# Fused attention and gated layer on one core: transfers and their issue moved, zero products added to the first maxima

## The chip, the cores and the metric

The kernel runs on one core of a Trainium2 chip. Its engines are TensorE (PE: matrix products into PSUM; PEld is its weight load), VectorE (DVE), ScalarE (ACT), GpSimd (POOL) and SyncE (SP). In this kernel SP only issues DMAs, POOL issues some as well. The engines run side by side, each in the order of its own instructions, and wait for each other by semaphores. The metric is the device time of one execution in microseconds, lower is better.

## The reference

```python
def _attn_ref(q, k, v):                       # 8 batches, 8 heads, 1152 rows, 64 columns
    q_pool = q.reshape(B, H, S // 2, 2, D).mean(axis=3)
    scores = scale * np.matmul(q_pool, k.transpose(0, 1, 3, 2))
    scores = scores - np.max(scores, axis=-1, keepdims=True)
    attn = np.exp(scores)
    attn = attn / (np.sum(attn, axis=-1, keepdims=True) + 1e-09)
    return np.matmul(attn, v)

def _moe_ref(x, w_in, w_out):                 # x: 4608 tokens x 512, w_in 512 x 2048, w_out 2048 x 512
    h = x @ w_in
    g = h - np.tanh(h)
    return g @ w_out
```

The attention's output, heads side by side, is x.

## The kernel before, in words

**Attention** goes over 32 pairs of heads (8 batches of 4 pairs), `pi` in the code. Keys and queries of a pair arrive as `raw` (SP, function `load`); ScalarE rounds them to a high part `hi` (tile kq_h, functions `high_keys` and `high`), and the low part `lo` (tile kq_l) comes from ScalarE's negative copy (`minus_high`) and an adding DMA on POOL's queue (`low`). In the same way `minus_keys` and the DMA of `differences` make differences of keys and sum the two halves of the queries. A product of scores is three products of high and low parts. Before a pair's scores, maxima of its rows are taken from products of the high parts alone: 12 by `max_part` (TensorE, then a VectorE reduction `mx`) and two by `max_last` for the last 64 rows of both heads, whose queries SP copies into a tile of their own, `q_last` (function `last_queries`, at the end of `high`). `max_row` brings the maxima by VectorE, `m_dram` and two DMAs into the row `m_row`, which the scores subtract by a product with `sel`. For pair 0 a product with `eye` (`turn`) does this instead.

The order of a pair is written out as a string of tokens. `A` and `B` are the scores of the two halves of the queries (9 tiles of keys each; ScalarE's exponential follows, POOL adds exponentials in threes), `V` the products with the values, `m`, `L` and `l` the maxima of a later pair (`L` and `l` are `max_last`), `O` the sums of exponentials (ScalarE's copy `s_s` follows), `R` the second `turn`. The number behind the colon is the PSUM bank, of which there are four; `bank_111` to `bank_114` in an order listing are banks 0 to 3. Everything else hangs on places: `add(pi, place, f)` runs f after score number `place` of pair pi, or, from NS = 18 on, after its V number place - 18. So the place of an `add` sets where f's instructions stand on every engine, SP's queue included. SP issues its DMAs in this order and stops at each one that has to wait.

**Weights.** `W` converts a tile of w_in or w_out, which come as 64-bit numbers, to a high and a low part, one tile a pair: loads w_raw and w_off, token `T` (`begin` by ScalarE, `finish` by VectorE, six instructions, two DMAs to wi_dram or wo_dram).

**Reciprocals and x.** The sums go to s_dram; once a batch is through, `fetch_sums` and `reciprocals` (VectorE) write r_dram. x of a chunk of 512 tokens is fetched from x_dram into `x_l`, the reciprocals, spread over 64 rows, into `x_r`; `times`, `high` and `low` scale it and split it. For the first chunk this is spread over pairs 17 to 24.

**The second part** goes over 9 chunks in 16 steps each (n counts them all): `hidden` (12 products into ps_h), `shrink` (ScalarE squares and tanh, VectorE a polynomial, POOL a mask), and two steps later `second` (12 products into ps_o) with the high and low part of g. The first two steps are done inside the last pair (token `H`, `early_step`), with their weights in the raw tiles (`first_weights`) and their temporaries in kq_h and kq_l tiles. The other weights (w tiles) take the memory that the attention's pools give back.

Of the kernel before, what the change touches and what calls it, by code (L numbers as in the profile page):

```python
# [20 lines left out]
VALUES = "V:1 T:2 " + "V:1 " * 8 + "V:3 " * 4 + "m:0 m:1 m:2 " + "V:3 " * 5 + "m:1 L:0 l:3 O:2"  # L21
FIRST = (
    "A0:0 m0:1 A1:2 m0:3 A5:0 m0:1 A6:2 L0:3 A2:0 l0:1 A3:2 R:3 A7:0 m:1 A8:2 A4:0 m:1 B0:3 B1:2 B2:0 m:1 B5:3 B6:2 "
    "m:1 B7:0 B3:3 B4:2 m:1 B8:3 " + "V:1 " * 3 + "m1:0 m1:2 m1:3 " + "V:1 " * 4 + "m1:3 m1:0 m1:2 " + "V:1 " * 2 +
    "V:3 " * 2 + "m1:0 L1:1 l1:2 " + "V:3 " * 4 + "m:0 m:1 m:2 " + "V:3 " * 3 + "m:1 L:0 l:3 O:2")
# [3 lines left out]
LAST_BUT_ONE = PLAN + "V:1 T:2 " + "V:1 " * 8 + "T:0 " + "V:3 " * 9 + "O:2"  # L29
LAST = PLAN.replace("A7:1 ", "T:3 A7:1 ", 1) + "H:0 " + "V:3 " * 9 + "H:2 " + "V:3 " * 9 + "O:3"  # L30
# [29 lines left out]
def attention_ffn_kernel(  # L60
# [15 lines left out]
    P = 128  # L76
# [48 lines left out]
    class X:  # L125
# [8 lines left out]
        def fetch(self):  # L134
            sp.dma_start(self.l.bitcast(F32), x_dram[:, :, self.t0:self.t0 + self.n].rearrange("c p t -> p c t"))
# [87 lines left out]
    with ExitStack() as actx:  # L223
# [151 lines left out]

        def turn(pi, ta, tb, to):
# [119 lines left out]
        def early_step(to, places):  # L496
# [6 lines left out]
            b = lop.tile([P, LQ], F32R, name="kq_l")  # L503
            part = [a[:, 512 * i:512 * (i + 1)] for i in range(4)]
            m = a[:, 2048:2176].bitcast(mybir.dt.uint8)
            s.own = ((*part, m, bank[places][:, s.f]), b[:, 0:512], b[:, 512:1024])
# [17 lines left out]
        for pi in range(n_pair):  # L524
            if pi >= 2:
# [4 lines left out]
                else:  # L530
                    add(*((0, NS + 2) if pi == 3 else (pi - 3, 8)), load, pi)
# [12 lines left out]
        def begin_x():  # L544
            x0.append(X(0))
            x0[0].fetch()
# [13 lines left out]
        for f in range(2):  # L560
            add(n_pair - 1, 4, first_weights, f, (0, 1), "raw")
# [26 lines left out]
        def follow(pi, tokens, seen):  # L588

            for tok in tokens.split():  # L590
# [9 lines left out]
                elif what == "T":  # L600
                    w = work[len(made)]
                    made.append(w)
                    if seen["V"]:
                        w.begin(to, act)
                        at.setdefault((pi, NS + seen["V"] + 1), []).insert(0, w.finish)
                    else:
                        w.begin(to, dve)
# [58 lines left out]
    for ci in range(len(chunks)):  # L666
# [9 lines left out]
        for f in range(NF):  # L676
# [17 lines left out]
            if n == 4:  # L694
                fetch_sums(B - 1)
            if n == 6:
# [54 lines left out]
```

## Time and profile before

| | |
|---|---|
| median of 3 runs | 1601.51 us (1601.18 to 1602.08) |
| profiled execution | 1597.87 us, its span 1596.1 us |
| TensorE busy | 1544.3 us, 97% of the span |
| VectorE, ScalarE, POOL busy | 73%, 61%, 70% |

The page gives the busy time of each engine. TensorE is the longest, but a share over the whole span hides single places where it stands still; these are found by windows and by the idle time that a timeline notes in brackets before an instruction, with what ended it. PEclk is the clock that the chip granted to TensorE, 1 for 2.4 GHz. A time of a DMA in the chain of waits is from its issue to its landing.

### The profile page before, as it was taken

The numbers are of one execution on the slowest core, as the hardware profiler recorded it, in microseconds if no ns is written. First come the engines' busy times: TensorE is split into PE (matmuls) and PEld (weight loads), VectorE is DVE, ScalarE is ACT, GpSimd is POOL, SyncE is SP. The second block draws the span as 40 slices with busy tenths as digits, with TensorE's granted clock in tenths as the row PEclk, the third lists the DMA queues.
The fourth block names the chain that finished last, engine by engine and source line by source line (L and its number), as shares of the span: only waits on it lengthen the run. The fifth ranks groups of instructions, "written<-read, shape, count | busy, mean of one in ns | idle before, by whom it ended". The sixth has DMA issues, their size and how long they took to land.

```text
span 1596.1 us, 29936 instructions
## 1 busy us (share of the span) xinstructions
PE 1544.3 (97%) x11505; PEld 1193.5 (75%) x11505; DVE 1165.8 (73%) x1643; ACT 974.7 (61%) x1634; POOL 1112.7 (70%) x812
## 2 busy tenths in 40 slices
PE   7899999999979999999887999999999999999998
PEld 5577677767757677677676888888888888888886
DVE  5677777777757777777556777777777777777776
ACT  6476677667656676676444556565565556565554
POOL 7477787788757787787545666666667576666664
PEclk9999999999989999999998999999999999999999
DMA  5677678767768778776571101011010201020000
GB/s 160 179 225 213 200 216 238 184 215 220 221 184 219 200 219 226 192 215 175 213 308 36 66 14 67 7 35 43 10 67 14 67 14 67 14 67 14 27 0 27
DMA packets 92360, 202.66 MB, mean 127 GB/s; under 512 B 18232, under 2 KB 45240, under 8 KB 92216
## 3 DMA queue, kind: packets, MB, share of 16 engines
q1 hardware_dynamic: 83288, 156.04, 27.2%
q0 software_dynamic: 8928, 44.70, 15.1%
q8 instruction: 90, 1.47, 0.4%
q14 instruction: 54, 0.44, 0.1%
HBM read 134.25 MB, written 37.98 MB: 108 GB/s over the span
## 4 chain that ended last, share of the span: by engine, by line
PE 90%; DMA 5%; DVE 2%; POOL 1%; ACT 1%; issue 1%; SPq 0%; POOLq 0%; DVEq 0%; ACTq 0%
PE bank L50 44%; PE ps_h L50 24%; PE ps_o L50 23%; DMA w<-wo_dram 2%; DVE mx L50 1%; DMA q_last<-kq_h 1%; POOL sum L50 1%; DMA m_dram<-tr 0%; DMA rec<-s_dram 0%; DMA kq_l<-raw 0%; SPq L50 0%; DVE bank L50 0%; DMA raw<-in_qk_dram 0%; DMA w_raw<-in_w_out_dram 0%; DVE w_hl L50 0%
## 5 line engine op out<-in xcount | busy, mean ns | idle before, releaser
L50 DVE TENSOR_REDUCE mx<-bank 128x2 f32<-128x768 f32 x448 | 401.0, 925 | 171.2 <-PE bank L50 157.8
L50 POOL TENSOR_SCALAR g_m<-g_u 128x512 uint8<-128x512 f32 (+1 forms) x143 | 248.4, 1737 | 198.0 <-ACT g_u L50 183.7
L50 POOL TENSOR_TENSOR sum<-p,p 128x576 f32<-128x576 f32 x192 | 272.2, 1424 | 152.2 <-ACT p L50 152.2
L50 ACT ACTIVATE p<-bank 128x576 f32<-128x576 f32 x576 | 328.4, 659 | 24.1 <-PE bank L50 20.1
L50 PE MATMUL bank<-kq_h 64*128 64x288 f32 (+1 forms) x1920 | 288.5, 344 | 8.4 <-ACT kq_h L50 6.5
L50 PE MATMUL bank<-p,v 128*64 128x288 f32 x2304 | 293.9, 409 | 0.3 <-DVE mx L50 0.3
L50 POOL TENSOR_TENSOR sum<-sum,p 128x576 f32<-128x576 f32 x192 | 273.1, 1429 | 12.5
L50 PE MATMUL ps_o<-w,g_hi 128*128 128x512 f32 x792 | 244.0, 389 | 1.0 <-ACT g_hi L50 1.0
L50 PEld LDWEIGHTS bank<-p,v 128*64 128x64 f32 x2304 | 159.3, 137 | 114.5 <-issue 12.9
L50 POOL TENSOR_TENSOR g_lo<-g_s,g_hi 128x512 fp32r<-128x512 f32 (+1 forms) x143 | 184.1, 1287 | 84.3 <-ACT g_hi L50 84.3
L50 PEld LDWEIGHTS bank<-kq_h 64*128 64x128 f32 x1920 | 170.9, 185 | 74.6 <-DVE mx L50 25.9
L50 PE MATMUL ps_h<-x_h,w 128*128 128x512 f32 (+1 forms) x800 | 213.2, 389 | 13.9 <-DVE g_t L50 13.9
L50 ACT ACTIVATE g_u<-ps_h 128x512 f32<-128x512 f32 (+1 forms) x143 | 84.6, 592 | 230.9 <-PE ps_h L50 229.2
L50 DVE SCALAR_TENSOR_TENSOR ps_w<-g_u,ps_h 128x512 f32<-128x512 f32 (+1 forms) x143 | 99.0, 692 | 141.3 <-ACT g_t L50 141.3
L50 ACT ACTIVATE g_s<-g_u,pc 128x512 f32<-128x512 f32 (+1 forms) x286 | 190.5, 714 | 11.1
L50 PEld LDWEIGHTS ps_h<-x_h,w 128*128 128x128 f32 x800 | 150.1, 189 | 45.2 <-DVE g_t L50 14.3
L50 PEld LDWEIGHTS ps_o<-w,g_hi 128*128 128x128 f32 x792 | 148.5, 188 | 32.1 <-ACT g_hi L50 1.4
L50 PE MATMUL bank<-kq_l,kq_h 64*128 64x288 f32 x1152 | 170.6, 293 | 0.0
L50 PE MATMUL bank<-kq_h,kq_l 64*128 64x288 f32 x1152 | 170.4, 292 | 0.0
L50 PE MATMUL ps_o<-w,g_lo 128*128 128x512 f32 x396 | 154.4, 390 | 0.6 <-POOL g_lo L50 0.5
L50 DVE COPY_PREDICATED g_s<-g_m,g_t 128x512 f32<-128x512 uint8 (+1 forms) x143 | 108.0, 755 | 14.7
L50 DVE SCALAR_TENSOR_TENSOR g_s<-g_s,ps_w 128x512 f32<-128x512 f32 (+1 forms) x143 | 97.7, 683 | 17.5 <-DVE ps_w L50 3.7
(111 smaller groups left out, 2339.1 us busy)
## 6 DMA issues: line engine op xcount, KB each, us to landing
raw<-in_qk_dram SPq DMA_DIRECT2D x31, 864.0 KB
kq_l<-raw POOLq DMA_DIRECT2D x31, 864.0 KB, 7.5
v<-in_v_dram SPq DMA_DIRECT2D x32, 576.0 KB
raw<-in_qk_dram POOLq DMA_DIRECT2D x31, 544.0 KB, 11.0
x_dram<-o_s SPq DMA_DIRECT2D x32, 288.0 KB
x_l<-x_dram SPq DMA_DIRECT2D x9, 1024.0 KB
out_dram<-o_f SPq DMA_DIRECT2D x36, 256.0 KB
w_raw<-in_w_in_dram SPq DMA_DIRECT2D x16, 512.0 KB
```

The source lines that it names most:

```text
L50: i = f(*args, **kwargs)
```

## The change

1. Pair 0: `minus_high` and `low` of pair 1 move from the first values (places 18 and 19) to the sixth and eighth score (5 and 7); the load of pair 3 from place 20 to 18. One maximum of pair 1 moves from the scores to the values.
2. Nine first maxima use three banks, not four, and behind each stand one or two `warm`, two products of zeros each, into bank 3 (28 in all).
3. Token `T` moves ahead of the first V, and `finish` with it by one V. In the last pair the token is `D` (VectorE begins, as before).
4. x of the first chunk is fetched in four parts in pairs 10, 12, 14 and 16; x_r at the end of pairs 16, 18, 20 and 22. Its product with x moves from the end of the values to their first place (`product`: ScalarE copies x_r to bank 0, VectorE multiplies), `high` from place 34 to 28.
5. The raw tiles' weights are loaded at place 31 of pair 30, not at place 4 of pair 31.
6. The second early step keeps its g in two x_r tiles, not in a kq_l tile.
7. Sums and reciprocals of the last batch move from steps 4 and 6 to 30 and 32.

```diff
-VALUES = "V:1 T:2 " + "V:1 " * 8 + "V:3 " * 4 + "m:0 m:1 m:2 " + "V:3 " * 5 + "m:1 L:0 l:3 O:2"
+VALUES = "T:2 " + "V:1 " * 9 + "V:3 " * 4 + "m:0 m:1 m:2 " + "V:3 " * 5 + "m:1 L:0 l:3 O:2"
...
+        def warm(to):
+
+            for h in range(2):
+                pe.matmul(bank[to][:, h], rows(columns, h)[:, 4], rows(columns, h)[:, 0:4].rearrange("p t n -> p (t n)"),
+                          start=True, stop=True)
...
-            b = lop.tile([P, LQ], F32R, name="kq_l")
+            if early:
+                g_h, g_l = (rt.tile([P, 512], F32R, name="x_r") for _ in range(2))
+            else:
+                b = lop.tile([P, LQ], F32R, name="kq_l")
+                g_h, g_l = b[:, 0:512], b[:, 512:1024]
...
-                    add(*((0, NS + 2) if pi == 3 else (pi - 3, 8)), load, pi)
+                    add(*((0, NS) if pi == 3 else (pi - 3, 8)), load, pi)
...
-        add(h_x, 2, begin_x)
+        add(h_x - 8, 2, begin_x)
+
+        def product(c):
+            x = x0[0]
+            t, holds[0] = bank[0][:, 0], None
+            act.activation(t, x.r[c], AF.Copy)
+            dve.tensor_tensor(x.r[c], x.l[:, c].bitcast(F32), t, op=ALU.mult)
         for c in range(NP):
-            add(h_x + 2 * c, 9, lambda c=c: x0[0].fetch_r(c))
-            add(h_x + 2 * c, NS + 15, lambda c=c: x0[0].times(dve, c))
-            add(h_x + 2 * c, NS + 16, lambda c=c: x0[0].high(c))
+            add(h_x - 7 + 2 * c, 14, lambda c=c: x0[0].fetch(c))
+            add(h_x + 2 * c - 1, NS + 14, lambda c=c: x0[0].fetch_r(c))
+            at[h_x + 2 * c, NS].insert(1, lambda c=c: product(c))
+            add(h_x + 2 * c, NS + 10, lambda c=c: x0[0].high(c))
...
-            add(n_pair - 1, 4, first_weights, f, (0, 1), "raw")
+            add(n_pair - 2, NS + 13, first_weights, f, (0, 1), "raw")
...
-            max_part(0, i, i % 4)
+            max_part(0, i, i % 3)
+            for n in range(1 if i < 4 else 2):
+                warm(3)
...
-        add(0, NS, minus_high, 1)
-        add(0, NS + 1, low, 1)
+        add(0, 5, minus_high, 1)
+        add(0, 7, low, 1)
...
-                    if seen["V"]:
-                        w.begin(to, act)
+                    w.begin(to, act if what == "T" else dve)
+                    if what == "T":
                         at.setdefault((pi, NS + seen["V"] + 1), []).insert(0, w.finish)
...
-            if n == 4:
+            if n == NF + 14:
                 fetch_sums(B - 1)
-            if n == 6:
+            if n == 2 * NF:
                 reciprocals(B - 1)
```

POOL's queue in pair 0, from the third addition of exponentials on (sum, p; kq_l is the low part, here of pair 1 and then of pair 2). Before:

```order
L50 TENSOR_TENSOR sum_1_275<-p_260,p_273 128x576
L50 TENSOR_TENSOR sum_1_275<-sum_1_275,p_287 128x576
L50 TENSOR_TENSOR sum_2_315<-p_302,p_313 128x576
L50 TENSOR_TENSOR sum_2_315<-sum_2_315,p_325 128x576
L50 TENSOR_TENSOR sum_0_352<-p_339,p_350 128x576
L50 DMA raw<-in_qk_dram 128x1088
L50 TENSOR_TENSOR sum_0_352<-sum_0_352,p_363 128x576
L50 TENSOR_TENSOR sum_1_389<-p_375,p_387 128x576
L50 TENSOR_TENSOR sum_1_389<-sum_1_389,p_400 128x576
L50 TENSOR_TENSOR sum_2_423<-p_411,p_421 128x576
L50 TENSOR_TENSOR sum_2_423<-sum_2_423,p_434 128x576
L50 DMA kq_l<-raw 128x1728 x2
```

Now:

```order
L50 TENSOR_TENSOR sum_1_303<-p_288,p_301 128x576
L50 TENSOR_TENSOR sum_1_303<-sum_1_303,p_315 128x576
L50 TENSOR_TENSOR sum_2_345<-p_332,p_343 128x576
L50 DMA kq_l<-raw 128x1728
L50 TENSOR_TENSOR sum_2_345<-sum_2_345,p_356 128x576
L50 TENSOR_TENSOR sum_0_383<-p_367,p_381 128x576
L50 DMA raw<-in_qk_dram 128x1088
```

The copy of pair 1 now stands seven additions earlier; that of pair 2 stays at the end.

SP's queue in pair 1, from the write of the maxima's row on (m_dram, m_row: of pair 2; q_last: of pair 3; w_hl: the converted weights). Before:

```order
L50 DMA m_dram<-tr 128x128
L50 DMA m_row_119<-m_dram 2x16x32
L50 DMA m_row_119<-m_dram 2x2x32
L50 DMA q_last_124<-kq_h 64x64 x2
L50 DMA wi_dram<-w_hl 128x4x128 x2
L50 DMA x_dram<-o_s 128x576
```

Now:

```order
L50 DMA m_dram<-tr 128x128
L50 DMA m_row_119<-m_dram 2x16x32
L50 DMA m_row_119<-m_dram 2x2x32
L50 DMA wi_dram<-w_hl 128x4x128 x2
L50 DMA q_last_124<-kq_h 64x64 x2
L50 DMA x_dram<-o_s 128x576
```

The two writes and the two copies have changed places, and so it is in each of the pairs 1 to 29.

SP's queue from the last tile of weights on (in_w_out_dram: its loads; wo_dram<-w_hl: its writes; raw<-wi_dram and raw<-wo_dram: weights of the two early steps). Before:

```order
L50 DMA wo_dram<-w_hl 128x512 x4
L50 DMA w_raw<-in_w_out_dram 128x2048
L50 DMA w_off<-in_w_out_dram 128x2048
L50 DMA x_dram<-o_s 128x576
L50 DMA s_dram<-s_s 4x288
L50 DMA wo_dram<-w_hl 128x512 x2
L50 DMA raw<-wi_dram 128x1024
L50 DMA raw<-wo_dram 128x1024
L50 DMA raw<-wi_dram 128x1024
L50 DMA raw<-wo_dram 128x1024
```

Now:

```order
L50 DMA wo_dram<-w_hl 128x512 x4
L50 DMA w_raw<-in_w_out_dram 128x2048
L50 DMA w_off<-in_w_out_dram 128x2048
L50 DMA raw<-wi_dram 128x1024
L50 DMA raw<-wo_dram 128x1024
L50 DMA raw<-wi_dram 128x1024
L50 DMA raw<-wo_dram 128x1024
L50 DMA x_dram<-o_s 128x576
L50 DMA s_dram<-s_s 4x288
L50 DMA wo_dram<-w_hl 128x512 x2
```

The four loads now stand ahead of the last tile's two writes.

## Rows read from the trace of the kernel before

**Rows 1.** Windows by stage: stretch, length, busy us of each engine, clock, DMA.

```profile
0.00:52.89 52.89, 34.94 (x267) 23.42 (x268) 30.62 (x46) 24.89 (x38) 28.80 (x32) 0.97 0.65 173
...
428.00:462.53 34.53, 25.31 (x256) 17.53 (x255) 18.19 (x25) 16.64 (x27) 18.56 (x14) 0.85 0.85 222
462.53:764.41 301.88, 300.59 (x3252) 217.23 (x3252) 230.24 (x312) 206.07 (x337) 238.76 (x179) 1.00 0.71 203
764.41:795.16 30.75, 26.60 (x252) 18.99 (x248) 14.02 (x22) 17.02 (x31) 17.16 (x12) 1.00 0.68 251
795.16:854.90 59.74, 45.84 (x192) 37.46 (x193) 31.79 (x47) 23.75 (x41) 23.76 (x16) 0.89 0.59 224
854.90:1596.10 741.20, 735.92 (x3253) 608.39 (x3251) 558.51 (x816) 429.50 (x744) 487.98 (x334) 1.00 0.10 34
```

**Rows 2.** Timeline of ScalarE, sums of pairs 16, 17, 18: start, length, instruction, [idle].

```profile
428.08 0.41 ACT L50 ACTIVATE s_s<-bank 128x288 f32<-128x288 f32 x1 [2.30 <-PE bank L50]
...
462.53 0.41 ACT L50 ACTIVATE s_s<-bank 128x288 f32<-128x288 f32 x1 [12.76 <-PE bank L50]
485.72 0.41 ACT L50 ACTIVATE s_s<-bank 128x288 f32<-128x288 f32 x1 [2.29 <-PE bank L50]
```

**Rows 3.** Timeline of TensorE in pair 0 and at the end of pair 13.

```profile
17.20 0.44 PE L50 MATMUL bank<-m_row,sel 64*128 64x288 f32 x2
...
22.43 0.29 PE L50 MATMUL bank<-m_row,sel 64*128 64x288 f32 x2
...
52.89 1.30 PE L50 MATMUL bank<-kq_h,q_last 128*128 128x384 f32 x3 [6.50 <-DMA q_last<-kq_h]
...
356.00 0.79 PE L50 MATMUL bank<-kq_h,q_last 128*128 128x384 f32 x3
```

**Rows 4.** Chain of waits up to 100 us: start, length, what.

```profile
38.61 6.18 DMA kq_l<-raw
```

**Rows 5.** Timeline of VectorE, first maxima.

```profile
7.28 7.87 DVE L50 TENSOR_REDUCE mx<-bank 128x2 f32<-128x768 f32 x9 [2.08 <-PE bank L50]
```

**Rows 6.** Timeline of ScalarE in pair 0.

```profile
17.81 0.64 ACT L50 ACTIVATE p<-bank 128x576 f32<-128x576 f32 x1
...
28.35 3.89 ACT L50 ACTIVATE p<-bank 128x576 f32<-128x576 f32 x7
...
33.00 1.64 ACT L50 ACTIVATE kq_l<-raw 128x1728 fp32r<-128x1728 f32 x1
```

**Rows 7.** Chain of waits from 430 to 470 us.

```profile
449.38 8.61 DMA q_last<-kq_h
```

**Rows 8.** Timelines of SP and POOL at the end of pair 13.

```profile
351.71 1.16 SPq L50 DMA_DIRECT2D q_last<-kq_h  x2
352.96 1.00 SPq L50 DMA_DIRECT2D wo_dram<-w_hl  x2
...
355.36 0.87 POOL L50 DMA_DIRECT2D kq_l<-raw  x1
```

**Rows 9.** Timelines of SP and TensorE at the end of pair 23.

```profile
597.86 1.16 SPq L50 DMA_DIRECT2D q_last<-kq_h  x2
...
600.73 0.62 PE L50 MATMUL bank<-kq_h,q_last 128*128 128x384 f32 x2
```

**Rows 10.** Timeline of TensorE, first early step.

```profile
777.39 1.17 PE L50 MATMUL bank<-x_h,raw 128*128 128x512 f32 x4 [2.74 <-DMA raw<-wi_dram]
```

**Rows 11.** Timelines of VectorE, SP, POOL and TensorE behind the last pair.

```profile
801.34 0.69 DVE L50 TENSOR_TENSOR kq_l<-kq_h,kq_l 128x512 fp32r<-128x512 f32 x1 [5.59 <-ACT kq_l L50]
...
806.41 0.32 SPq L50 DMA_DIRECT2D w<-wi_dram  x1
...
842.23 1.26 POOL L50 TENSOR_TENSOR x_r<-x_l,x_r 128x512 f32<-128x512 f32 x1 [12.42 <-DMA x_r<-r_dram]
...
847.43 2.08 PE L50 MATMUL ps_h<-x_h,w 128*128 128x512 f32 x4 [13.90 <-DVE g_t L50]
```

**Rows 12.** The page's costliest groups: instruction xcount | busy us, mean ns | idle.

```profile
L50 ACT ACTIVATE g_s<-g_u,pc 128x512 f32<-128x512 f32 (+1 forms) x286 | 190.5, 714 | 11.1
```

More of the change, by code (lines that the diff above doesn't have):

```diff
@@ L20 @@
 STARTS = 5
-VALUES = "V:1 T:2 " + "V:1 " * 8 + "V:3 " * 4 + "m:0 m:1 m:2 " + "V:3 " * 5 + "m:1 L:0 l:3 O:2"
+VALUES = "T:2 " + "V:1 " * 9 + "V:3 " * 4 + "m:0 m:1 m:2 " + "V:3 " * 5 + "m:1 L:0 l:3 O:2"
 FIRST = (
-    "A0:0 m0:1 A1:2 m0:3 A5:0 m0:1 A6:2 L0:3 A2:0 l0:1 A3:2 R:3 A7:0 m:1 A8:2 A4:0 m:1 B0:3 B1:2 B2:0 m:1 B5:3 B6:2 "
-    "m:1 B7:0 B3:3 B4:2 m:1 B8:3 " + "V:1 " * 3 + "m1:0 m1:2 m1:3 " + "V:1 " * 4 + "m1:3 m1:0 m1:2 " + "V:1 " * 2 +
-    "V:3 " * 2 + "m1:0 L1:1 l1:2 " + "V:3 " * 4 + "m:0 m:1 m:2 " + "V:3 " * 3 + "m:1 L:0 l:3 O:2")
+    "A0:0 m0:1 A1:2 m0:3 A5:0 m0:1 A6:2 L0:3 A2:0 l0:1 A3:2 R:3 A7:0 m:1 A8:2 A4:0 B0:3 m:1 B1:2 B2:0 B5:3 m:1 B6:2 "
+    "B7:0 B3:3 m:1 B4:2 B8:3 " + "V:1 " * 2 + "m1:0 m1:2 m1:3 " + "V:1 " * 5 + "m1:3 m1:0 m1:2 " + "V:1 " * 2 +
+    "V:3 " * 2 + "m1:0 L1:1 l1:2 m1:0 " + "V:3 " * 4 + "m:0 m:1 m:2 " + "V:3 " * 3 + "m:1 L:0 l:3 O:2")
 PLAN = (
@@ L28 @@
     "A8:0 m:3 ")
-LAST_BUT_ONE = PLAN + "V:1 T:2 " + "V:1 " * 8 + "T:0 " + "V:3 " * 9 + "O:2"
-LAST = PLAN.replace("A7:1 ", "T:3 A7:1 ", 1) + "H:0 " + "V:3 " * 9 + "H:2 " + "V:3 " * 9 + "O:3"
+LAST_BUT_ONE = PLAN + "T:2 " + "V:1 " * 9 + "T:0 " + "V:3 " * 9 + "O:2"
+LAST = PLAN.replace("A7:1 ", "D:3 A7:1 ", 1) + "H:0 " + "V:3 " * 9 + "H:2 " + "V:3 " * 9 + "O:3"
 PLAN += VALUES
@@ L132, in __init__, with fetch @@
             self.r = {}
-        def fetch(self):
-            sp.dma_start(self.l.bitcast(F32), x_dram[:, :, self.t0:self.t0 + self.n].rearrange("c p t -> p c t"))
+        def fetch(self, c=slice(0, NP)):
+            src = x_dram[c, :, self.t0:self.t0 + self.n]
+            sp.dma_start(self.l[:, c].bitcast(F32), src if isinstance(c, int) else src.rearrange("c p t -> p c t"))
         def fetch_r(self, c):
@@ L502, in early_step @@
             a = hip.tile([P, KQ], F32R, name="kq_h").bitcast(F32)
-            b = lop.tile([P, LQ], F32R, name="kq_l")
+            if early:
[3 more added lines that the diff above has]
+                g_h, g_l = b[:, 0:512], b[:, 512:1024]
             part = [a[:, 512 * i:512 * (i + 1)] for i in range(4)]
             m = a[:, 2048:2176].bitcast(mybir.dt.uint8)
-            s.own = ((*part, m, bank[places][:, s.f]), b[:, 0:512], b[:, 512:1024])
+            s.own = ((*part, m, bank[places][:, s.f]), g_h, g_l)
             shrink(s, early[-1] if early else None)
@@ L599, in follow @@
                     run(pi, NS + seen["V"] - 1)
-                elif what == "T":
+                elif what in "TD":
                     w = work[len(made)]
                     made.append(w)
-                    if seen["V"]:
-                        w.begin(to, act)
+                    w.begin(to, act if what == "T" else dve)
+                    if what == "T":
                         at.setdefault((pi, NS + seen["V"] + 1), []).insert(0, w.finish)
                     else:
-                        w.begin(to, dve)
                         w.finish()
```

1 line of the change is left out of this document (removed).

## The prediction

> **What bounds the kernel now.** I read the stages first [rows 1]: busy time of each engine in stretches that begin and end where TensorE passes from one part to another. Its idle time is a stretch's length less its busy time. In the end stage from 854.90 it idles 5.3 of 741 us, from 462.53 to 764.41 1.3 of 302. The time that can be won lies in four places: 17.95 us idle up to 52.89, 9.22 between 428 and 462.53, 4.15 between 764.41 and 795.16, and 13.90 between 795.16 and 854.90. In the second and the fourth the granted clock is also below 1 (0.85, 0.89), so work done there is slower too. Next I read the ladder of one instruction that occurs once a pair, ScalarE's copy of the sums [rows 2]: a pair takes 23.19 us (462.53 to 485.72), but pair 17 takes 34.45, so that one place costs 11.26 us. Then the timelines of TensorE and of what it waited for, place by place. The change touches all four, and it also alters the order on SP's queue in every pair.
>
> **Start, stall of pair 0.** TensorE waits 6.50 us for q_last of pair 2, at 52.89 [rows 3]. The copy was queued on SP behind the load of pair 3, which had to wait until POOL's accumulating copy kq_l of pair 1, issued at 38.61, had landed 6.18 us later [rows 4]. The change moves that copy to the eighth score. Its input on ScalarE follows the sixth, and POOL by then has four additions before it, so I put the issue at about 26 and the landing at about 33 with the same 6 to 7 us. The load of pair 3 then goes at 33, q_last follows ScalarE's high part of pair 2 (near 37), and L is due near 43: the 6.5 us go. With them goes work at the lower clock level: three products took 1.30 us after the stall (at 52.89) and take 0.79 in an ordinary pair (at 356.00) [rows 3]; the sums behind them ran low as well, so 1.5 us in all is my estimate.
>
> **Start, zero products.** Until about 22 TensorE runs at the lower level, 1.2 GHz: a step of two products took 0.44 us at 17.20 and 0.29 at 22.43 [rows 3]. The granted figure of the stretch does not show this, the durations do. Before, TensorE had worked in short bursts beside nine maxima of VectorE (7.28 to 15.15 [rows 5]). The change puts 28 zero products between these bursts. They cost nothing as long as TensorE keeps ahead of VectorE's 0.87 us a maximum. At the lower level a maximum's pair takes about 0.32 us and a zero pair of 512 columns 0.43 (384 and 512 columns over 1.2 GHz), so 0.75 for the first four and 1.18 for the last five: if the level never rises, up to 1.5 us is lost, less what the two buffers in hand absorb (about 0.7). If it rises by 16, as I expect from nearly continuous work since about 7, the scores that follow are paced by ScalarE. From the first exponential at 17.81 to the end of the last, where kq_l begins at 33.00 [rows 6], ScalarE needs 18 of 0.56 us (3.89 for 7) and two small copies, some 11.2 of 15.2 us; 4 are idle. The moved kq_l (1.64) takes part of that. I take 2.5 us from here, bounds -1.5 and 4.
>
> The Trainium skill, TensorE: Matmul & The Clock Gate, Part 1, says that the chip's observation of activity does not begin anew with a kernel, so the point at which the clock rises varies from run to run. No run here shows that yet; by that rule part of the 2.5 us could be missing in some runs, and the rival below with no rise covers it.
>
> **Start, what is late next.** One more maximum of pair 1 now stands in the part of the values, which VectorE paces there: 0.4 us after the earlier start of that part. Its row of maxima then reaches SP near 41, just after POOL has issued kq_l of pair 2; such a copy took 6 us, so the row comes near 48, while the first scores of pair 1 want it near 46. I charge 2 us. The start sums to 6.5 + 1.5 + 2.5 - 0.4 - 2 = 8.1; bounds 4 (no rise of the clock, 2 us more wait) and 11.5 (no new wait).
>
> **Pair 17 and the three like it.** At 449.38 q_last is issued and takes 8.61 us [rows 7], since 1 MB of x on the DMA engines has held up what stands ahead of it on SP, so that it goes just behind two copies of POOL's. The change fetches x in four quarters, in pairs 10, 12, 14 and 16, and the reciprocal sums at the end of pairs 16, 18, 20 and 22. Each is 0.26 MB, about 0.7 us of DMA at the rate of 360 GB/s that rows 11 give (12.8 MB from 806.41 to 842.23). The four products move from the end of the values to their head, with 0.6 us more on ScalarE and 0.7 on VectorE, both of which have slack there. Gain: 34.45 - 23.19 = 11.3, and up to the 1.29 us idle from 462.53 to 764.41 [rows 1]: 12.5.
>
> **Every pair: q_last behind the weights' writes.** The W tile's conversion starts one value step earlier, and so its two writes now stand ahead of both q_last copies on SP. In an ordinary pair the copies were issued from 351.71 to 352.87 and the writes from 352.96 to 353.96, L began unhindered at 356.00 [rows 3, 8]. Swapped, the copies are issued at about 352.8 to 354.0, since the conversion, too, ends earlier than it did. How long they need is bounded from above by a tighter pair: issued until 599.02, first product at 600.73 without a wait, 1.71 us at most [rows 9]. So they land by 355.7, 0.3 before they are wanted, if the 0.5 MB of writes ahead does not hold them. I charge nothing in 21 ordinary pairs and 0.2 us in the eight that carry x or its sums, 1.6 us; bounds 0 and 14.5 (0.5 us in all 29).
>
> The Trainium skill, DMA: Bandwidth & Descriptors, section Queues, rings and completion order, says that a DMA engine alternates between the queues that have work, a packet at a time. By that rule a small copy on SP's queue would wait for a packet of POOL's, not for the whole; the 8.61 us of rows 7, issued just behind two POOL copies, shows that this can still be long. By the rule alone the sum is the same.
>
> **First weights.** TensorE waits 2.74 us before 777.39 for the raw tiles' weights [rows 10], whose loads stood on SP behind the last W tile's writes. Now they stand ahead of them; by the same rate their 2.1 MB need 6 us from 765 on, and the first is due at 774.65. Gain 2.7.
>
> **End of attention, the 13.9 us.** VectorE stood at the reciprocals of the last batch, and TensorE waited 13.90 us for it, until 847.43 [rows 11]. The change moves sums and reciprocals a whole chunk later, so VectorE's wait goes. But POOL waited just as long, 12.42 us until 842.23, for x_r of the next chunk [rows 11], and ScalarE's copy to x_h reads what POOL makes of it, 1.26 later; these stay in place, ahead of the activations of the ninth step. What is late next is therefore x_r, which comes last of the 12.8 MB that SP sends from 806.41 on without a gap. The first of these loads waits, by the program's order, for the second early step's product, which reads its g from the kq_l tile. With that g in the x_r tiles, the memory is free when VectorE's last g_low ends, 801.34 + 0.69 [rows 11]: 4.4 us sooner. In the old times x_h then starts at 839.2. The copy, four activations and g_hi take 3.5 us (some 0.6 each, 0.7 for g_s [rows 12]), so g_hi is there at 842.7. TensorE stopped at 833.5 (847.43 less 13.90); it now has one hidden part of 2.7 us more to do and stands from 836.2 to 842.7. After 6.5 us idle its clock is low again, as after the 6.50 us of rows 3. From 847.43 to 854.90 24 products took 7.5 us instead of 5.4, so the first 12 some 4.8; with half a microsecond for g_lo the next hidden part begins at 848.0, not at 854.90. Gain 6.9; bounds 2.6 (loads no sooner) and 16 (x_r hidden).
>
> **Sum.** 8.1 + 12.5 - 1.6 + 2.7 + 6.9 = 28.6. The profiled execution took 1597.87 us (span 1596.1 and 1.77 around it), the median shown is 1601.51, 3.6 more. 1597.9 - 28.6 = 1569.3 profiled, 1572.9 as a median: 1573.
>
> **Rivals.**
> 1. The zero products do not raise the clock before the scores: the start gives about 4, time 1577. For it: the bursts before did not raise it. Against: with them TensorE works nearly without a gap. 0.15.
> 2. x_r is no longer late, or the wait is short, since the loads start far sooner: 9 us more, 1564. Against: POOL's wait does not depend on the reciprocals. 0.12.
> 3. q_last comes a little late in each of 29 pairs, 0.3 us: 8.7 less what I charged, 1580. For: margin of only 0.3 us. 0.15.
> 4. Slower: q_last slips behind POOL's copies of the same pair (issued 355.36 [rows 8], 1.4 us after my end of its issue). Then the wait of pair 17 returns, 11.3 us a pair. From three pairs on this outweighs the gain; in the four pairs with extra sums it gives 1573 + 45 = 1618. Against: the order within a pair repeats within some tenths. 0.06.
> 5. The loads start no sooner, because the pool's release still waits for another reader: 4.3 less, 1577. 0.05.
>
> My forecast has the remaining 0.47. Bounds added up would be 1556 to 1601; the range that leaves out 2 in 10 is 1562 to 1587. What this kernel's measurement can tell from no change is about 0.2%, 3.2 us. Slower by more than that needs rival 4: 0.06. Within it needs two or three of the losses at once: 0.02. Faster: 0.92.
>
> **What would show it.** In the profile after: no wait for q_last at pair 0, and the copy of sums of pair 0 near 46 instead of 56.83; products of 0.29 us a step from 16 on; a ladder with no step over 24 us; no wait before the first x_h product; first w load about 4 us sooner after it; POOL still waiting for x_r, TensorE idle 5 to 8 us once near 830 (in the new time, some 25 us earlier than 836). Wrong would be: steps of 23.5 or more all along the ladder with waits for q_last (rivals 3, 4), or products of 0.44 us until 22 (rival 1).

## The result, and the profile after

The changed kernel takes 1576.07 us (median of 4 runs, 1573.94 to 1576.47), the kernel before 1601.8 us beside it: ratio 0.9837, 95% interval 0.982 to 0.9854. That is 25.7 us less; 1573 (1562 to 1587) was predicted. The profiled execution took 1575.8 us, its span 1573.8 us against 1596.1 before, so the two traces compared below differ by 22.3 us.

Where these lie is read from ScalarE's copy of the sums, once a pair, as in [rows 2]. From its timeline before (start, length, instruction, [idle]), the copies of pairs 0, 1, 30 and 31 (those of 16 and 17 stand in [rows 2]):

```profile
56.83 0.41 ACT L50 ACTIVATE s_s<-bank 128x288 f32<-128x288 f32 x1 [3.45 <-PE bank L50]
80.03 0.41 ACT L50 ACTIVATE s_s<-bank 128x288 f32<-128x288 f32 x1 [2.29 <-PE bank L50]
...
764.55 0.41 ACT L50 ACTIVATE s_s<-bank 128x288 f32<-128x288 f32 x1 [1.27 <-PE bank L50]
794.70 0.41 ACT L50 ACTIVATE s_s<-bank 128x288 f32<-128x288 f32 x1 [1.86 <-PE bank L50]
```

The same timeline after, pairs 0, 1, 16, 17, 30 and 31:

```profile
48.52 0.41 ACT L50 ACTIVATE s_s<-bank 128x288 f32<-128x288 f32 x1 [2.33 <-PE bank L50]
76.59 0.41 ACT L50 ACTIVATE s_s<-bank 128x288 f32<-128x288 f32 x1 [2.29 <-PE bank L50]
...
424.51 0.41 ACT L50 ACTIVATE s_s<-bank 128x288 f32<-128x288 f32 x1 [3.06 <-PE bank L50]
447.75 0.41 ACT L50 ACTIVATE s_s<-bank 128x288 f32<-128x288 f32 x1 [2.29 <-PE bank L50]
...
749.38 0.41 ACT L50 ACTIVATE s_s<-bank 128x288 f32<-128x288 f32 x1 [1.25 <-PE bank L50]
777.79 0.41 ACT L50 ACTIVATE s_s<-bank 128x288 f32<-128x288 f32 x1 [1.86 <-PE bank L50]
```

Differences of these starts, and what the prediction said of the same stretch:

| stretch | before | after | gained | predicted |
|---|---|---|---|---|
| start to the copy of pair 0 | 56.83 | 48.52 | 8.3 | 10.1 |
| pair 0 to 1 | 23.20 | 28.07 | -4.9 | -2 |
| pair 1 to 16 | 348.05 | 347.92 | 0.1 | -1.6 over pairs 1 to 30 |
| pair 16 to 17 | 34.45 | 23.24 | 11.2 | 12.5, of it 11.3 here |
| pair 17 to 30 | 302.02 | 301.63 | 0.4 | the rest of the 12.5 |
| pair 30 to 31 | 30.15 | 28.41 | 1.7 | 2.7 |
| pair 31 to the end | 801.4 | 796.0 | 5.4 | 6.9 |
| sum | | | 22.3 | 28.6 |

What TensorE and its weight load (PEld) still wait for, after (waited for: us in total, times, longest us):

```profile
PE ps_o L50 <- ACT g_hi L50: 8.2, 2, 7.2
...
PE bank L50 <- DMA q_last<-kq_h: 3.8, 4, 1.3
PE bank L50 <- DMA m_row<-m_dram: 3.4, 1, 3.4
...
PEld bank L50 <- DVE w_hl L50: 0.9, 4, 0.2
```

Three things stand there: one long wait in the second part, a wait for the row of maxima in pair 1 that was not there before, and q_last in four pairs. The last row, PEld's wait for VectorE's conversion of a W tile, was 4.8 us in 25 pairs before:

```profile
PEld bank L50 <- DVE w_hl L50: 4.8, 25, 0.2
```

The prediction's sum did not have this wait. TensorE at the start, after (start, length, instruction, [idle]):

```profile
8.98 0.52 PE L50 MATMUL bank<-kq_h 64*128 64x384 f32 x2
9.83 0.34 PE L50 MATMUL bank<-kq_h 64*128 64x384 f32 x2
...
14.77 0.55 PE L50 MATMUL bank<-eye,columns 128*128 128x128 f32 x3 [1.99 <-DVE columns L50]
...
17.09 0.45 PE L50 MATMUL bank<-m_row,sel 64*128 64x288 f32 x2
...
20.63 0.29 PE L50 MATMUL bank<-m_row,sel 64*128 64x288 f32 x2
...
40.15 0.80 PE L50 MATMUL bank<-kq_h,q_last 128*128 128x384 f32 x3 [0.97 <-ACT o_s L50]
...
46.06 0.79 PE L50 MATMUL bank<-kq_h,q_last 128*128 128x384 f32 x3
...
52.78 0.40 PE L50 MATMUL bank<-m_row,sel 64*128 64x288 f32 x2 [3.37 <-DMA m_row<-m_dram]
```

Two products of q_last stand there. The one at 40.15 is for pair 1 (it did not wait for q_last before either). The one for pair 2, which had waited 6.50 us until 52.89 [rows 3], stands at 46.06 and waits for nothing. Without its wait it would have stood at 46.39 before, so the work ahead of it came only 0.3 us sooner. What held it up is read from ScalarE's copy of the queries' sums of pair 2. Before:

```profile
36.28 1.11 ACT L50 ACTIVATE kq_h<-raw 128x1088 fp32r<-128x1088 f32 x1 [0.60 <-DMA raw<-in_qk_dram]
```

After:

```profile
37.15 1.11 ACT L50 ACTIVATE kq_h<-raw 128x1088 fp32r<-128x1088 f32 x1 [3.83 <-DMA raw<-in_qk_dram]
```

ScalarE was ready 2.4 us sooner (33.3 against 35.7) and could start 0.9 us later. The DMA it waits for (POOL's `differences`) was issued at 30.35, hardly sooner than before (30.63), and took 6.72 us. Behind this copy comes ScalarE's `o_s`, for which TensorE waits at 40.15.

The clock rose sooner than forecast, during the maxima (0.34 us a pair at 9.83, where the pairs up to 8.98 took 0.52), and then fell: the same step takes 0.45 at 17.09 and 0.29 at 20.63. And pair 1 begins with a wait of 3.37 us. What it waits for, from the chain of waits after (the first line is the DMA of `differences` named above, the second the row):

```profile
30.35 6.72 DMA raw<-in_qk_dram
43.81 6.48 DMA m_dram<-tr
```

The row goes to m_dram at 43.81, takes 6.48 us, and only then can it come back as m_row, some 2 us more.

The end of attention, after; the first weights' load on SP, POOL's x_r and ScalarE's x_h, TensorE (timelines of the four engines):

```profile
785.27 0.32 SPq L50 DMA_DIRECT2D w<-wi_dram  x1
...
821.74 1.26 POOL L50 TENSOR_TENSOR x_r<-x_l,x_r 128x512 f32<-128x512 f32 x1 [8.82 <-DMA x_r<-r_dram]
...
823.04 0.63 ACT L50 ACTIVATE x_h<-x_r 128x512 fp32r<-128x512 f32 x1 [11.50 <-POOL x_r L50]
...
826.57 1.22 PE L50 MATMUL ps_o<-w,g_hi 128*128 128x512 f32 x2 [7.22 <-ACT g_hi L50]
```

The stall of 13.90 us [rows 11] is now 7.22 us, and its end hangs on x_r, through POOL, x_h and g_hi, as forecast.

### The profile page after: what moved, and what is told of

It is laid out like the page before. It is cut to its first block, busy times and chain, and to the rows that moved or that the text cites. A ratio compares the mean times of both kernels' runs of the same rounds, so it can differ in the third digit from the quotient of the medians.

```text
span 1573.8 us, 30012 instructions
## 1 busy us (share of the span) xinstructions
PE 1540.5 (98%) x11533; PEld 1194.9 (76%) x11533; DVE 1153.0 (73%) x1643; ACT 977.0 (62%) x1638; POOL 1120.5 (71%) x812
## 4 chain that ended last, share of the span: by engine, by line
PE 90%; DMA 5%; DVE 2%; ACT 1%; SPq 1%; issue 1%; POOL 0%; POOLq 0%; ACTq 0%; DVEq 0%
PE bank L50 43%; PE ps_h L50 23%; PE ps_o L50 23%; DMA w<-wi_dram 2%; DVE mx L50 1%; SPq L50 1%; DMA q_last<-kq_h 1%; DMA raw<-in_qk_dram 1%; DMA m_dram<-tr 1%; DMA x_r<-r_dram 1%; DMA raw<-wo_dram 0%; DVE w_hl L50 0%; ACT g_s L50 0%; DVE bank L50 0%; POOL sum L50 0%
## 5 line engine op out<-in xcount | busy, mean ns | idle before, releaser
L50 POOL TENSOR_SCALAR g_m<-g_u 128x512 uint8<-128x512 f32 (+1 forms) x143 | 252.3, 1764 | 196.0 <-ACT g_u L50 181.7
L50 POOL TENSOR_TENSOR sum<-p,p 128x576 f32<-128x576 f32 x192 | 277.9, 1453 | 145.5 <-ACT p L50 145.5
L50 PE MATMUL bank<-kq_h 64*128 64x288 f32 (+1 forms) x1920 | 285.3, 340 | 7.7 <-ACT kq_h L50 5.8
L50 POOL TENSOR_TENSOR sum<-sum,p 128x576 f32<-128x576 f32 x192 | 272.5, 1426 | 12.5
L50 DVE COPY_PREDICATED g_s<-g_m,g_t 128x512 f32<-128x512 uint8 (+1 forms) x143 | 108.1, 756 | 15.1 <-DVE g_t L50 0.5
L50 PEld LDWEIGHTS bank<-kq_l,kq_h 64*128 64x128 f32 x1152 | 110.0, 187 | 0.0
```

Source lines behind the costliest of these rows:

```text
L50: i = f(*args, **kwargs)
```

## The experiments

Unless said otherwise each is the changed kernel with one edit; in the diffs `...` marks lines left out. The kernel before, measured beside each, had medians of 1600.9 to 1601.7 us. The executions of one kernel spread over 1 to 6 us, so a difference under 2 us between two kernels is not read from the times. Stages are compared by the profiles, one per kernel, and these scatter too. In the nine kernels that have the start as changed, zero products included, the copy of sums of pair 1 comes at 75.4 to 77.0 us. In the seven that have the end as changed, the part behind the last copy of sums takes 794.4 to 796.2 us.

**Without the zero products.**

```diff
-            for n in range(1 if i < 4 else 2):
-                warm(3)
```

> The changed kernel without its 28 zero products. In the profile of the changed kernel the step of two products is 0.34 us from 9.8 to 11.3, then 0.45 again until 19.2, and 0.29 from 20.1. Theory: the products raised the clock only during the maxima, the wait for the maxima's row let it fall, and the second rise came 2 us sooner than before; without them the copy of sums of pair 0 comes about 1 us later than 48.52 and the time rises by 1 us, to 1577. Rival as predicted: they are worth 2.5 us, 1578.6. Second rival: they are worth nothing, because the row of maxima of pair 1 is what pair 1 waits for: 1576.

Measured: 1574.54 us (1572.21 to 1576.78), no longer than with them. In the profile they do something. Without them the clock stays low to about 21 (the step takes 0.44 at 18.04, 0.29 at 21.93), the copy of pair 0 comes at 49.90 and that of pair 1 at 77.99, 1.4 us later each than with them. Of this, 0.3 us stands at TensorE's first product already (6.10 against 5.80), and this profile is the longest of its four executions. Against the nine kernels with them, 77.99 is 1.0 to 2.6 us late. So a worth of 1 to 2.5 us is an estimate from one profile without them; the theory's 1 us and the 2.5 of its rival both lie in it, and the times don't show it. In the profile the last rival falls, since pair 1 is later too; by the times it would stand.

**POOL's copies at place 1 of pair 1,** meant to stand behind the first addition.

```diff
-                    add(pi - 2, 0, differences, pi)
-                for at_, f in zip(late, (high_keys, high, minus_high, low)):
+                    if pi == 3:
+                        add(1, 1, low, 2)
+                    add(pi - 2, int(pi == 3), differences, pi)
+                for at_, f in zip(late, (high_keys, high, minus_high, low)[:3 if pi == 2 else 4]):
```

> Of the changed kernel, POOL's two copies at the end of pair 0 (kq_l of pair 2, differences of pair 3) are issued behind the first addition of pair 1. Theory: these copies hold up the row of maxima of pair 1, whose first part took 6.48 us from 43.81; without them it takes 2 to 3 us, TensorE's wait of 3.4 us for m_row goes, the step from the copy of sums of pair 0 to that of pair 1 falls from 28.07 to 24 or less, and the time by 4, to 1572. Rival: other traffic (the load of pair 3, landed about 40) holds it; the wait stays, 1576. Second rival: the delayed copies come late for the copy to kq_h of pair 3 or for the scores of pair 2, and what is gained is lost there: 1576 or more.

Measured: 1575.93 us, a second step of 28.06 us, POOL's copies at 40.55 and 41.69. The edit did not do what it says: the first addition stands behind the third score, so place 1 is still ahead of it and POOL's queue is that of the changed kernel. It tells nothing about the theory; it is a second measurement of the changed kernel (1576.07).

**The same copies at place 2.**

```diff
-                    add(pi - 2, 0, differences, pi)
+                    add(pi - 2, 2 * (pi == 3), differences, pi)
+                    if pi == 3:
+                        add(1, 2, low, 2)
...
```

> Of the changed kernel, POOL's two copies at the end of pair 0 (kq_l of pair 2 and differences of pair 3, issued at 40.10 and 41.31) now stand behind the first addition of pair 1 in POOL's program, which they did not yet in the kernel e2. Theory: they hold up the row of maxima of pair 1 (first part 6.48 us from 43.81, TensorE's wait 3.37 us, the step from the copy of sums of pair 0 to that of pair 1 28.07 instead of 23.07). With the copies issued near 49 instead, the first part takes 2 to 3 us, the wait goes, the step is 24 or less, the time 4 us shorter: 1572. Rival: the load of pair 3 and other traffic hold the row, and the wait stays: 1576. Second rival: the copies, 9 us later, make the copy to kq_h of pair 3 or the scores of pair 2 late, and what is gained is lost there, as a step over 24 in pair 2: 1576 or more.

Measured: 1584.31 us (1582.34 to 1586.12), 8 slower. SP's timeline, from the row of pair 1 on:

```profile
42.88 0.33 SPq L50 DMA_DIRECT2D m_dram<-tr  x1
44.46 1.22 SPq L50 DMA_DIRECT2D m_row<-m_dram  x2
...
62.08 0.34 SPq L50 DMA_DIRECT2D raw<-in_qk_dram  x1
...
63.47 0.65 SPq L50 DMA_DIRECT2D m_dram<-tr  x1
69.39 1.08 SPq L50 DMA_DIRECT2D m_row<-m_dram  x2
```

The first part of the row of pair 1 is through 1.58 us after its issue, not 6.48, and the wait for m_row is gone: POOL's copies were the cause. But the time was lost again: the load of pair 4 stood on SP until 62.08, because it overwrites what the DMA of kq_l of pair 2, issued at 52.59 now, reads; behind it the row of pair 2 took 5.9 us and q_last came behind POOL's next copies. TensorE in pair 1 of this kernel:

```profile
81.65 1.30 PE L50 MATMUL bank<-kq_h,q_last 128*128 128x384 f32 x3 [13.21 <-DMA q_last<-kq_h]
```

The second rival had the sign right, but the place it named (a copy to kq_h or the scores of pair 2) was not the one.

**x of the second chunk sooner.** The weights from the eleventh load on are loaded behind x_l and the first x_r.

```diff
...
+    load_all(range(10))
...
                     nxt.fetch_r((4, 5, 9, 11).index(f))
+                if n == 4:
+                    load_all(range(10, NF))
```

> Of the changed kernel, the 1 MB load of x and the first x_r load of the second chunk stand on SP behind ten loads of weights instead of behind all 22. Theory: x_r came last of the loads, and the stall of 7.22 us at 826.57 with the first 12 products behind it at the lower clock level (5.65 us instead of 2.72) is that alone; both go, 10 us: 1566. Rival: with x_r there, another link of the same chain is late (the weights behind it, or ScalarE's copy to x_h and the activations), 3 to 5 us are won: 1572. Second rival: the loads behind x slow those of the weights that TensorE needs next, nothing is won: 1576.

Measured: 1563.89 us (1563.63 to 1565.86), 12.2 less. From the last copy of sums to the end it is 785.6 us instead of 796.0, so 10.3 lie there. POOL's timeline:

```profile
812.04 1.30 POOL L51 TENSOR_TENSOR g_lo<-g_s,g_hi 128x512 fp32r<-128x512 f32 x1 [0.31 <-ACT g_hi L51]
813.30 1.29 POOL L51 TENSOR_TENSOR x_r<-x_l,x_r 128x512 f32<-128x512 f32 x1
```

x_r follows the work before it with no wait, and TensorE has none behind 778.67 but 1.0 us for g_hi and 0.5 for g_lo. The stall of 7.2 us went whole, and with it the low clock behind it (the 12 products there took 5.65 us, now 2.72). So x_r's place in SP's queue was the cause; nothing else came late in its place.

**The writes of the W tile behind q_last,** its conversion where the change put it.

```diff
+            def write(self):
...
                         at.setdefault((pi, NS + seen["V"] + 1), []).insert(0, w.finish)
+                        at.setdefault((pi, NS + seen["V"] + 2), []).insert(0, w.write)
...
```

> Of the changed kernel, the W tile is converted where the change put it, one value step sooner than before, but its two writes are issued a value step later, behind both q_last copies, as before. In the changed kernel an ordinary pair takes 23.07 us instead of 23.20, and five pairs take 23.6 to 24.4 with waits for q_last. Theory: the 0.13 us come from the sooner conversion, the five waits from the writes ahead of q_last; so the ordinary pair stays at 23.07 and the waits go, 4.4 us: 1571.7. Rival: the 0.13 us come from the order on SP; the pair is back at 23.20, the waits go: 3.3 us lost, 4.4 won, 1575. Second rival: the waits are those of pairs that carry loads of x or of sums, and stay: 1576.

Measured: 1570.44 us (1570.2 to 1572.4), 5.6 less. The ordinary pair stays at 23.07 and TensorE waits for q_last nowhere. The slowest pair of the changed kernel (24.41) in its timelines of SP, POOL and TensorE:

```profile
510.35 0.93 SPq L50 DMA_DIRECT2D wi_dram<-w_hl  x2
511.37 1.26 SPq L50 DMA_DIRECT2D q_last<-kq_h  x2
...
514.34 0.87 POOL L50 DMA_DIRECT2D kq_l<-raw  x1
...
516.05 0.77 PE L50 MATMUL bank<-kq_h,q_last 128*128 128x384 f32 x3 [1.31 <-DMA q_last<-kq_h]
```

and on SP in this experiment, same pair:

```profile
507.85 1.16 SPq L50 DMA_DIRECT2D q_last<-kq_h  x2
509.10 2.05 SPq L50 DMA_DIRECT2D wi_dram<-w_hl  x2
```

From pair 1 to 30 it takes 669.0 us (75.67 to 744.71), 3.7 less than the changed kernel (672.8). That is the price of the writes ahead of q_last. It varies: the six other kernels with the writes ahead and the pairs else as changed take 671.4 to 674.4 us for this stretch, the four with the writes behind 668.9 to 669.4.

**The conversion of the W tile as before.**

```diff
-VALUES = "T:2 " + "V:1 " * 9 + "V:3 " * 4
+VALUES = "V:1 T:2 " + "V:1 " * 8 + "V:3 " * 4
...
-LAST_BUT_ONE = PLAN + "T:2 " + "V:1 " * 9
+LAST_BUT_ONE = PLAN + "V:1 T:2 " + "V:1 " * 8
```

(Each of these four lines goes on as it was.)

> Of the changed kernel, the conversion of the W tile begins behind the first value step again, as before, so that its arithmetic ends and its writes are issued one step later (behind q_last). Theory: the ordinary pair goes back from 23.07 to 23.20 us, since VectorE's conversion then stands in front of the first maxima of the part of the values, 25 pairs of 0.13, 3.3 us; and the waits for q_last go, as in the kernel with the writes behind (4 to 5.6 us won). Together 1573.5, about 3 more than that kernel's 1570.4. Rival: the shorter pair comes from something else in the change (x no longer multiplied there, the loads at other points); the ordinary pair stays at 23.07 and the time is 1570.4.

Measured: 1575.5 us (1574.51 to 1578.18), 5.1 more than the kernel above. Pair 1 to 30 takes 674.0 us, 5.0 more, an ordinary pair 23.23. TensorE at the first maxima of the values, this kernel:

```profile
371.80 0.97 PE L50 MATMUL bank<-kq_h 64*128 64x384 f32 x6
```

and the changed kernel:

```profile
371.44 0.80 PE L50 MATMUL bank<-kq_h 64*128 64x384 f32 x6
```

With the conversion one V later, VectorE does it just when the bank of these maxima is wanted, and each pair pays 0.16 us. So the sooner conversion is worth 5.0 us, and its writes took 3.7 of them back. The theory holds, at 5.0 instead of 3.3.

**x of the first chunk as before** (part 4 of the change undone).

```diff
+            x0[0].fetch()
...
-        add(h_x - 8, 2, begin_x)
+        add(h_x, 2, begin_x)
...
-            add(h_x - 7 + 2 * c, 14, lambda c=c: x0[0].fetch(c))
-            add(h_x + 2 * c - 1, NS + 14, lambda c=c: x0[0].fetch_r(c))
-            at[h_x + 2 * c, NS].insert(1, lambda c=c: product(c))
-            add(h_x + 2 * c, NS + 10, lambda c=c: x0[0].high(c))
+            add(h_x + 2 * c, 9, lambda c=c: x0[0].fetch_r(c))
+            add(h_x + 2 * c, NS + 15, lambda c=c: x0[0].times(dve, c))
+            add(h_x + 2 * c, NS + 16, lambda c=c: x0[0].high(c))
```

> Of the changed kernel, x and the reciprocal sums are fetched, and x multiplied, where the kernel before did it (one load of 1 MB in pair 17, products at the end of the values); all else stays. Theory: the stall of pair 17 is the 1 MB load's alone, so it returns: one step of about 34.5 us in the ladder instead of 23.2, and the time rises by 10 to 12.5 us, to 1586 to 1588. Rival: in the changed kernel the writes stand ahead of q_last, which is later still behind POOL's copies, and the stall is longer than before (more than 36 us): 1590. Second rival: another part of the change already removed the stall (the sooner conversion moves q_last's issue): no step over 26, 1576 to 1579.

Measured: 1589.04 us (1586.82 to 1592.82), 13 more; pair 17 takes 36.54 us and pair 19 29.03. Its chain of waits in pair 17:

```profile
445.83 9.37 DMA q_last<-kq_h
```

The first rival is right: the stall is x's, and longer than before, 36.5 us against 34.45. Behind the writes q_last is issued 1.3 us later in its pair than before, and it takes 0.8 us longer. The pairs 2 to 16 are free of slow steps in this kernel, so the small waits there come from the quarters of x together with the writes.

**The second early step's g as before** (part 6 undone).

```diff
-                g_h, g_l = (rt.tile([P, 512], F32R, name="x_r") for _ in range(2))
...
+            b = lop.tile([P, LQ], F32R, name="kq_l")
+            g_h, g_l = b[:, 0:512], b[:, 512:1024]
```

> Of the changed kernel, the g of the second early step lies again in a kq_l tile instead of two x_r tiles. Theory: the release of the attention's memory then waits for the second early product, so the first of the 22 loads goes 4 us later behind the last copy of sums (11.7 us instead of 7.5), x_r with it, and TensorE's stall at the ninth step grows from 7.2 to about 11: 1580. Rival: that tile is not what the release waits for, the loads start as in the changed kernel: 1576.

Measured: 1578.51 us (1577.4 to 1582.26). The first load of weights goes at 788.11, 11.7 us behind the last copy of sums (7.5 with the change), the stall is 10.61 us, the part behind the last copy of sums 3.8 us longer (799.8; 3.5 to 5.4 against the seven kernels named at the head). The theory holds, with 3.8 for 4.

**Sums and reciprocals of the last batch as before** (part 7 undone).

```diff
-            if n == NF + 14:
+            if n == 4:
                 fetch_sums(B - 1)
-            if n == 2 * NF:
+            if n == 6:
                 reciprocals(B - 1)
```

> Of the changed kernel, the sums of the last batch are fetched and their reciprocals taken in the first chunk again (fifth and seventh step) instead of the second. Theory: they are one of two waits that end together; x_r of the next chunk comes as late as the sums, so the reciprocals add only VectorE's queue behind them, the one hidden part that TensorE can no longer do ahead: 2.7 us, 1579. Rival: VectorE's wait is the whole difference between a stall of 13.9 and one of 7.2 us, and returns in full: 1583. Second rival: x_r alone decides, nothing changes: 1576.

Measured: 1577.37 us (1573.55 to 1579.54); behind the last copy of sums 796.9 us, 0.9 more than with the change (0.6 to 2.5 against the seven kernels). VectorE and TensorE in it:

```profile
821.25 1.24 DVE L50 TENSOR_SCALAR rec<-rec 128x36 f32<-128x36 f32 x1 [10.76 <-DMA rec<-s_dram]
...
826.40 2.08 PE L50 MATMUL ps_h<-x_h,w 128*128 128x512 f32 x4 [9.29 <-DVE g_t L50]
```

The releaser named by the trace is VectorE, as in [rows 11], and yet taking this wait away is worth 0.9 us: x_r ends at the same moment (POOL's product with it starts at 821.19), and behind it the same chain. The second rival is nearest.

**x sooner and writes behind, together** (the two diffs above in one kernel).

> Of the changed kernel, x of the second chunk is loaded behind ten loads of weights, and the writes of the W tile stand behind q_last: the two edits that each won alone (12.2 and 5.6 us). Theory: they lie in different stages and add up: 1576.1 - 12.2 - 5.6 = 1558.3. Rival: what is won in the pairs comes back as a longer wait at the end (the weights' loads start at a fixed point behind the last pair, so nothing should): 1561 or more.

Measured: 1560.96 us (1560.33 to 1563.04), ratio to before 0.975 (0.9736 to 0.9763). The last copy of sums comes at 773.31 (773.09 with the writes alone), the rest takes 785.6 us (785.6 with x alone). So the two edits add up stage by stage, 4.5 + 10.3 = 14.8 us, and 15.1 by the medians. The 17.8 expected were differences of medians that exceed what the profiles give (9.9 for x alone, 4.9 for the writes alone), most likely by the scatter of the runs.

**Then POOL's copies of pair 2 and 3, kq_l first.**

```diff
-                    add(pi - 2, 0, differences, pi)
+                    if pi == 3:
+                        add(1, 2, low, 2)
+                    add(pi - 2, 2 * (pi == 3), differences, pi)
...
```

> The kernel with x sooner and the writes behind q_last, and with POOL's two copies at the end of pair 0 behind the first addition of pair 1, kq_l of pair 2 ahead of the differences of pair 3. With them behind in the other order, the row of maxima came at once (first part landed 1.6 us after 42.88) but the load of pair 4 waited on SP until 62.08 for kq_l, and TensorE 13.2 us for q_last behind it. Theory: with kq_l first that load goes 4 us sooner, near 58, and with the writes behind it q_last is issued ahead of POOL's next copies: the second step of the ladder falls from 28 to 23.5 to 25, 3 to 4.5 us less than the kernel without this edit: 1554. Rival: the queue of SP is still late (load of 0.9 MB and two of 0.5 MB ahead of the row of pair 2), a stall of 5 to 13 us in pair 1 or 2 comes in place of the wait for m_row: 1560 to 1568.

Measured: 1565.38 us (1564.04 to 1566.01), 4.4 more than the kernel above. The load of pair 4 goes at 60.72, the row of pair 2 is held from 62.14 to 69.58, and q_last comes 6.41 us late. The rival is right.

**Then also the load of pair 4 behind q_last.**

```diff
-                    add(*((0, NS) if pi == 3 else (pi - 3, 8)), load, pi)
-                    add(pi - 3, NS + 12, minus_keys, pi)
+                    add(*((0, NS) if pi == 3 else (1, NS + 2) if pi == 4 else (pi - 3, 8)), load, pi)
+                    add(pi - 3, 2 * NS if pi == 4 else NS + 12, minus_keys, pi)
```

> The kernel with kq_l of pair 2 behind the first addition, and with the load of pair 4 on SP behind the row of maxima, q_last and the writes of pair 2 (and ScalarE's negated copy of its keys behind the sums). There the load of pair 4 waited on SP for kq_l until 60.72, and with the two weight loads behind it held the first part of the row of pair 2 from 62.14 to 69.56; q_last came 6.4 us late. Theory: that load in SP's queue is the price; with it behind, the row of pair 2 goes near 63 and lands at once, no wait of either kind stays in pairs 0 to 2, the second step of the ladder is 23 to 24: 4 to 5 us less than the kernel with x sooner and writes behind, 1556 to 1557. Rival: raw of pair 4 is then late for its own copies (negated keys, differences, high part), and the stall moves to pair 2: 1561 or more.

Measured: 1558.68 us (1557.85 to 1563.11), ratio 0.9735 (0.9722 to 0.9749). The waits for m_row and q_last are gone. But the second step is 27.33 us, not 23 to 24 as expected. The profiled execution was the longest of its five (1563.11), and ScalarE waits in it for the queries' sums of pairs 2 and 3 (start, length, instruction, [idle]):

```profile
38.15 1.11 ACT L51 ACTIVATE kq_h<-raw 128x1088 fp32r<-128x1088 f32 x1 [5.31 <-DMA raw<-in_qk_dram]
...
67.77 1.11 ACT L51 ACTIVATE kq_h<-raw 128x1088 fp32r<-128x1088 f32 x1 [3.68 <-DMA raw<-in_qk_dram]
```

The first of these waits is not new: it was 3.83 us in the changed kernel, at 37.15. The second is, so here again a later link came in place of the wait that was removed. By the median it is 2.3 us less than the kernel with x and the writes; the two intervals overlap, so which of these two is faster is left open. Both beat the changed kernel by 15 to 17 us.

## Why the prediction was right, and where not

The time was 3 us off and within the range. The sum was off by more: it gave 28.6 us between the traces, which hold 22.3. The median of before was 3.6 us above its profiled execution, and I carried this over; but the profile of before lay at the short end of its executions (36 later ones have spans of 1597.1 to 1601.2 us, the profiled one 1596.1), and that of the changed kernel lies at its median. So 3 of the 6 us cancelled, and that the time came out so close is in part luck. The prediction's "bounds added up" of 1556 to 1601 do not follow from the bounds it states: these give 1559 to 1594.

**Start: failed, 3.4 for 8.1, below the lower bound of 4.** (The nine kernels with this start give 3.0 to 4.6 by the copy of pair 1.) Right was the main step: kq_l of pair 1 issued at 26.99, behind five additions and not four, the load of pair 3 at 33.28, no wait for q_last. The 6.5 us are there, and the 1.5 of low clock behind them too: from the product of q_last to the copy of pair 0 it took 3.94 us before and 2.46 after.

Two steps failed. The first is a wait that the sum put at nothing: of the 2.5 us from the zero products, less 0.4 for the moved maximum, 0.3 arrived at the product of q_last. ScalarE was ready 2.4 us sooner and then stood 3.83 us for the queries' sums of pair 2 (above). That their DMA was slower because the moved kq_l was still under way (issued at 26.99; SP's load that waits for it went at 33.28) fits, but no run separates it.

The second is the size of "what is late next", the "2 us" charged for the row of pair 1. It was put at SP near 41, 6 us, "near 48". It came at 43.81, and after the 6.48 us to m_dram there is the second DMA back to m_row, which the sum left out; then low clock for some 3 us behind the wait of 3.37 (the step took 0.50 from 53.84 to 56.80). Together 4.9. The experiment with POOL's copies behind the addition shows the cause (1.58 us for the same DMA). In the three kernels that removed this wait, others came in its place, so none of them got the 4.9 us.

**Zero products: right in direction, the size open (an estimate of 1 to 2.5 us for 2.5).** The clock rose in the maxima already. Then TensorE paused for the maxima's columns, 1.3 to 2 us. In 3 of 12 profiles of kernels with zero products the clock then fell, in 9 it stayed. Where it rose varies as well: the first maximum at 0.34 us stands at 9.8 to 12.7 us in the twelve. That the point of the rise varies is what the Trainium skill, TensorE: Matmul & The Clock Gate, Part 1, was cited for, and here the traces agree. The first rival (no rise before the scores) was wrong, but in the profile of the changed kernel, one of the three, the scores up to 20 us ran at the lower level as that rival had it.

**Pair 17: right,** 11.2 us there. The undone edit costs 13 us, more than before: pair 17 is 2 us longer, behind the writes, and pair 19 takes 29.03 us (23.84 before), which no run explains.

**q_last behind the writes: the mechanism right, the size not.** TensorE waited for it in four pairs, 0.7 to 1.3 us each, not in eight for 0.2; 3.7 us for 1.6, inside the bounds. Rivals 3 and 4 did not occur: q_last was issued ahead of POOL's copies of its pair. The margin was thin: in three of the four pairs the issue of its second copy ended within 0.25 us of the moment when POOL's began. What the sum did not have is the gain of 5.0 us from the conversion's new place. It was in the profile of before as PEld's 25 waits of 0.2 us for w_hl; I had read only TensorE's own waits, which don't show it. The two errors cancelled.

**First weights: 1.7 for 2.7.** The load is on time; the last exponential of pair 31 is next (0.96 us for p ahead of the first x_h product).

**The end: right in mechanism, 5.4 for 6.9.** The loads go 4.2 us sooner (4.4 forecast); x_r came 3.6 us sooner, since the same 22 loads took a little longer. The stall was 7.2 us (6.5), the 12 products behind it 5.65 (4.8). The split was off: the lower bound of 2.6 credited the reciprocals with that much, and undone alone they cost 0.9. Rival 2 (x_r not late) was wrong, and rival 5 too.

## What to carry to other kernels

When a wait is removed, follow what it let through all the way to its last leg: here a row of maxima goes through two DMAs, and both count. A releaser in a profile is the last of several; the reciprocals were named for 13.9 us and were worth 0.9, the load that ended at the same moment 10. What stood last in the queue of loads set the wait here, so order a queue by when each piece is wanted, not by kind: moving two loads of x ahead of weights that were wanted later gave by the medians (12.2 of 25.7 us) half as much as the whole change did.

## What the runs showed that was not expected

The granted clock and the durations tell different things at the start. Windows of the changed kernel and of the one with x sooner, from 16 to 20 us (stretch, length, busy us and count of PE, PEld, DVE, ACT, POOL, clock, DMA share, GB/s):

```profile
16.00:20.00 4.00, 4.00 (x30) 3.59 (x30) 2.87 (x3) 3.04 (x5) 1.62 (x2) 0.57 0.74 252
```

```profile
16.00:20.00 4.00, 3.74 (x40) 2.86 (x38) 3.32 (x4) 3.31 (x6) 1.75 (x2) 1.00 0.71 247
```

With 0.57 granted a step takes 0.45 us, with 1.00 0.29. But the figure is 1.00 in this stretch also before and without the zero products, while the step takes 0.44 there [rows 3]. Before:

```profile
16.00:20.00 4.00, 4.00 (x30) 3.88 (x31) 1.67 (x2) 2.68 (x4) 0.30 (x1) 1.00 0.65 229
```

So ahead of the first rise only the durations told the level in these profiles; after the fall the figure did show it.

A copy of 64 rows of queries needs 1.7 us or less when it is issued ahead of POOL's two copies of a pair [rows 9] and 8.6 to 9.4 us just behind them (8.61 in [rows 7], 9.37 in the kernel with x as before). The same copy took five times as long by the moment of its issue alone.
